# Moving one batch's x matmuls, its copies and two orderings in a fused attention and MLP kernel

## The chip, the cores and the metric

The kernel runs on one core of one Trainium2 chip. The metric is the device time of one execution in microseconds, as the median of several executions. A profile is one execution recorded by the hardware. Its span is about 1.8 us shorter than the time of the same execution (280.7 us against 282.54 us for the kernel before).

The engines are TensorE (PE in the profile), VectorE (DVE), ScalarE (ACT), GpSimd (POOL) and SyncE (SP), which here issues most of the DMA transfers (115 of the 120 that --dma lists for the kernel before). "L535" means line 535 of that kernel's own file.

## The reference, cut

There are 8 batches of 576 rows. Each batch goes through an attention that has no score matrix, then through a normalized two-layer MLP with a residual.

```python
def _attn_ref(q, k, v):                      # each (8, 8, 576, 64)
    q_s = exp(q - max(q, -1)); q_s /= sum(q_s, -1)
    k_s = exp(k - max(k, 2));  k_s /= sum(k_s, 2)
    kv = np.einsum('bhsd,bhse->bhde', k_s, v)
    return np.einsum('bhsd,bhde->bhse', q_s, kv)

def _moe_ref(x, g_ln, w_ch1, w_ch2):         # x (8, 576, 512), w_ch1 (512, 2048), w_ch2 (2048, 512)
    xn = (x - mean(x)) / np.sqrt(var(x) + 1e-06) * g_ln
    return x + np.maximum(xn @ w_ch1, 0.0) @ w_ch2
```

## The kernel before: the parts that matter

The MLP is done in nine chunks: the first 512 rows of each batch (chunks 0 to 7), and the last 64 rows of all batches together (chunk 8). While TensorE works on the MLP of chunk c, the other engines prepare batch c+1:

- ScalarE takes the exponentials of q and k (`eq`, `ek`) and casts v (`vb`).
- A DMA transposes `eq` into `eqT`.
- TensorE forms `kv`, and from `eqT` the transposed x. These are "the x matmuls": eight of 64x512, then eight of 64x64 for the last 64 rows.
- The results are copied out as `xsT`, which the chunk's first layer reads.
- Another DMA transposes `xsT` back to `x`, which the row statistics (`bn_stats` into `bst`) and the residual need.

Nothing is issued in program order. Every operation is entered in a plan, and a list scheduler orders the operations on each engine:

```python
    def add(self, eng, dur, fn, r=(), w=(), cls=1, land=0.0, mb=0.0, after=(), slack=0.0):
        ...                                   # deps: from the keys read (r) and written (w)
        order_only = set(after) - deps        # only shapes the plan; makes no data dependence
        self.tasks.append((eng, dur, fn, deps | order_only, (cls, i), ...))
```

An `after` holds an operation back in the plan. On one engine that fixes its place in the instruction order. Between two engines the built program waits only for data.

The casts of v, and the copies of the x matmuls' results:

```python
        def values(hf, s):
            ...
                plan.add("ACT", act_t(QW), lambda: nc.scalar.copy(vd, va), r=sk(s), w=[...],
                         cls=cls, slack=late, after=exps)

        def xT(hs):                           # 4 x matmuls for each h, then copies
            ...
                    if not steady and i == 1:
                        ev.append(plan.add("DVE", dve_t(512), lambda ...: nc.vector.tensor_copy(xt[:, g], pv), ...))
                    else:
                        ev.append(plan.add("ACT", act_t(512), lambda ...: nc.scalar.copy(xt[:, g], pv), ...))
```

The statistics of a chunk's x wait for the transposition. They stand on VectorE wherever the scheduler puts them:

```python
    def tokens(c, cls=1, after=()):
        i = plan.add("SP", 2.2, lambda: nc.sync.dma_start_transpose(x..., src...), r=r, w=[(xk, j) for j in range(J)], ...)
        for j in range(J):
            plan.add("DVE", dve_t(512), lambda j=j: nc.vector.bn_stats(bst[:, j, :], x[:, j, :]), r=[(xk, j)], ...)
            ...
```

From chunk 1 on, the second layer has seven products of half-size blocks. It uses sums `S` of the hidden blocks and sums `T` of w2's blocks. The second of its four output steps frees the PSUM bank that the last product needs:

```python
        product("S3", "T3", ga, False, False)
        final(o2, 1, ga, 2, 1)                # VectorE: ot <- pg (bank of ga), cp
        product("S4", "22", gb, False, True)
        final(o1, 1, gb, 1, 0)
        product("22", "T4", ga, False, True)  # TensorE needs ga's bank back
```

Chunk 0 has a plain second layer of 64 large matmuls. The sums `T` are formed meanwhile, 4 of the 16 on GpSimd:

```python
        for k0 in range(0, KO2, 4):
            for j in range(J):
                ...                           # four 128x512 matmuls
        ...
    def w2_sums(k0, n):
        ...
            eng, e = ("POOL", nc.gpsimd) if i == 2 else ("DVE", nc.vector)
            plan.add(eng, ..., lambda: e.tensor_tensor(T[i][:, ks], a, b, op=ALU.subtract), r=r, w=tk(i), cls=2)
```

The softmax here doesn't subtract the row's maximum and nothing guards it: scores larger than these inputs give would overflow.

## Time and profile before

| | before |
|---|---|
| median of 3 runs at the time of the prediction | 281.96 us (281.94 to 282.53) |
| median of 4 runs, beside the changed kernel | 282.12 us |
| TensorE busy, engine table | 269.3 of 280.7 us |
| VectorE, ScalarE, GpSimd busy | 205.1, 163.9, 12.6 us |

TensorE bounds this kernel almost everywhere. What a reordering can win is the idle time that is left on it, so the profile is read by stage. The first view of the kernel before is the table of stretches, cut at the starts of chunks 1, 2 and 3 on TensorE. Its columns are the stretch, its length, the busy time of each engine, the granted TensorE clock, the DMA share and GB/s.

```profile
37.30:55.00 17.70, 15.98 (x153) 7.29 (x152) 17.13 (x32) 8.40 (x13) 5.00 (x4) 1.00 1.10 293
55.00:83.40 28.40, 27.94 (x265) 18.07 (x263) 23.73 (x49) 24.10 (x35) 0.00 (x0) 1.00 0.95 288
83.40:113.40 30.00, 28.16 (x273) 17.98 (x266) 22.81 (x49) 19.90 (x34) 0.00 (x0) 1.00 0.81 191
113.40:276.00 162.60, 162.60 (x1402) 105.41 (x1400) 112.37 (x232) 87.73 (x150) 0.00 (x0) 1.00 0.52 138
```

The last stretch has no idle time on TensorE. The second layer of chunk 0 (first line, from 37.30 us) lacks 1.7 us, chunk 1 lacks 0.5 us and chunk 2 lacks 1.8 us.

Next comes TensorE's timeline of the kernel before: start, duration, line, operation, output and inputs, array tile, shape, count, and in brackets the idle time before the group with what ended it.

```profile
49.14 0.63 PE L405 MATMUL pa<-eqT,kve 64*64 64x512 bf16 x8 [1.23 <-DMA eqT<-eq]
49.70 1.04 PE L677 MATMUL pg<-w_sb,hT 128*128 128x512 f16 x4
50.66 0.22 PE L428 MATMUL pa<-eqT,kve 64*64 64x64 bf16 x2
51.37 0.25 PE L428 MATMUL pa<-eqT,kve 64*64 64x64 bf16 x6 [0.49 <-DVE xsT L416]
51.55 3.63 PE L677 MATMUL pg<-w_sb,hT 128*128 128x512 f16 x16
55.01 1.24 PE L535 MATMUL pa<-xsT,w_sb 128*128 128x512 f16 x5
```

The same timeline of the kernel before, at the ends of chunks 1 and 2:

```profile
81.38 1.91 PE L615 MATMUL pg<-T,hT 128*128 128x256 f16 x16 [0.41 <-DVE ot L625]
...
83.41 9.78 PE L535 MATMUL pg<-xsT,w_sb 128*128 128x512 f16 x44
...
107.90 1.91 PE L615 MATMUL pg<-w_sb,S 128*128 128x256 f16 x16
111.65 1.91 PE L615 MATMUL pg<-T,hT 128*128 128x256 f16 x16 [1.84 <-DVE ot L625]
113.39 0.81 PE L535 MATMUL pg<-xsT,w_sb 128*128 128x512 f16 x3
```

The four brackets are the four gaps of the prediction: A (1.23), B (0.49), C (0.41) and D (1.84). The cause of D is on VectorE, whose timeline of the kernel before shows a statistics instruction that waits for x ahead of the output step (`ot`) that TensorE needs:

```profile
106.35 0.88 DVE L625 SCALAR_TENSOR_TENSOR cp<-pg,st,x 128x256 f32<-128x256 f32 x2 [0.87 <-PE pg L615]
110.12 0.69 DVE L487 BATCH_NORM_STATS2 bst<-x 128x6 f32<-128x512 f16 x1 [2.89 <-DMA x<-xsT]
110.73 0.86 DVE L625 SCALAR_TENSOR_TENSOR ot<-pg,st,cp 128x256 f32<-128x256 f32 x2
```

Both casts of v wait for their loads, and they stand ahead of the copies of `xsT`:

```profile
79.59 1.17 ACT L368 CAST vb<-stg 128x1152 f16<-128x1152 f32 x1 [0.32 <-DMA stg<-in_v_dram]
81.03 1.17 ACT L368 CAST vb<-stg 128x1152 f16<-128x1152 f32 x1 [0.27 <-DMA stg<-in_v_dram]
82.10 1.06 ACT L418 CAST xsT<-pa 128x512 f16<-128x512 f32 x2
```

GpSimd's sums of w2, in the timeline of the kernel before:

```profile
43.14 2.45 POOL L566 TENSOR_TENSOR T<-w_sb 128x512 f16<-128x512 f16 x2 [17.28 <-DVE w_sb L301]
46.55 2.55 POOL L566 TENSOR_TENSOR T<-w_sb 128x512 f16<-128x512 f16 x2 [0.96 <-DVE w_sb L301]
```

### The profile page before, as it was taken

The numbers are of one execution on the slowest core, as the hardware profiler recorded it, in microseconds if no ns is written. First come the engines' busy times: TensorE is split into PE (matmuls) and PEld (weight loads), VectorE is DVE, ScalarE is ACT, GpSimd is POOL, SyncE is SP. The second block draws the span as 40 slices with busy tenths as digits, with TensorE's granted clock in tenths as the row PEclk, the third lists the DMA queues.
The fourth block names the chain that finished last, engine by engine and source line by source line (L and its number), as shares of the span: only waits on it lengthen the run. The fifth ranks groups of instructions, "written<-read, shape, count | busy, mean of one in ns | idle before, by whom it ended". The sixth has DMA issues, their size and how long they took to land.

```text
span 280.7 us, 5656 instructions
## 1 busy us (share of the span) xinstructions
PE 269.3 (96%) x2317; PEld 163.8 (58%) x2317; DVE 205.1 (73%) x408; ACT 163.9 (58%) x267; POOL 12.6 (5%) x17
## 2 busy tenths in 40 slices
PE   8988898999999997999999999999999999999994
PEld 3443344445864486546854785478447844874583
DVE  0988999899869874986598659966986683641573
ACT  3567793298887594569655865695565067006500
POOL 2115007000000000000000000000000000000000
PEclk9999999999999999999999999999999999999998
DMA  6999999999958992569655995797543650013004
GB/s 190 386 388 386 390 388 202 313 297 258 385 186 149 251 354 63 149 145 381 141 149 104 388 177 149 156 392 122 149 86 21 131 149 2 0 36 116 1 2 151
DMA packets 58522, 55.36 MB, mean 197 GB/s; under 512 B 37248, under 2 KB 37760, under 8 KB 58496
## 3 DMA queue, kind: packets, MB, share of 16 engines
q1 hardware_dynamic: 57776, 54.86, 68.6%
q8 instruction: 18, 0.29, 0.4%
q10 hardware_dynamic: 720, 0.13, 0.3%
q14 instruction: 8, 0.07, 0.1%
HBM read 36.70 MB, written 9.44 MB: 164 GB/s over the span
## 4 chain that ended last, share of the span: by engine, by line
PE 73%; DMA 13%; DVE 9%; ACT 1%; POOL 1%; issue 1%; DVEq 0%
PE pg L535 37%; PE pg L615 28%; DMA stg<-in_moe_w_ch_dram 6%; DMA x<-xsT 5%; PE pg L677 3%; DVE T L566 2%; DMA stg<-in_q_dram 2%; DVE S L551 2%; DVE bst L487 1%; PE pa L379 1%; PE pa L615 1%; PE pa L535 1%; POOL w_sb L271 1%; DVE ot L625 1%; PE pa L405 1%
## 5 line engine op out<-in xcount | busy, mean ns | idle before, releaser
L498 ACT ACTIVATE hT<-pg 128x512 f16<-128x512 f32 x134 | 79.4, 596 | 73.4 <-PE pg L535 72.6
L535 PE MATMUL pg<-xsT,w_sb 128*128 128x512 f16 x488 | 108.1, 379 | 0.5 <-DVE w_sb L292 0.5
L535 PEld LDWEIGHTS <-w_sb 128*128 128x128 f16 x568 | 54.8, 98 | 65.6 <-DVE w_sb L292 1.5
L615 PEld LDWEIGHTS <-S 128*128 128x128 f16 x512 | 49.7, 98 | 5.9
L615 PEld LDWEIGHTS <-hT 128*128 128x128 f16 x384 | 37.0, 98 | 10.5 <-issue 5.0
L615 PE MATMUL pg<-T,S 128*128 128x256 f16 x368 | 42.5, 273 | 0.1
L551 DVE TENSOR_TENSOR S<-hT 128x1024 f16<-128x1024 f16 x32 | 22.0, 688 | 25.9 <-ACT hT L498 25.8
L625 DVE SCALAR_TENSOR_TENSOR cp<-pg,st,x 128x256 f32<-128x256 f32 x46 | 20.2, 479 | 13.7 <-PE pg L615 12.9
L615 PE MATMUL pg<-w_sb,hT 128*128 128x256 f16 x248 | 29.3, 273 | 0.0
L625 DVE SCALAR_TENSOR_TENSOR ot<-pg,st,cp 128x256 f32<-128x256 f32 x47 | 20.5, 478 | 9.9 <-PE pg L615 9.7
L487 DVE BATCH_NORM_STATS2 bst<-x 128x6 f32<-128x512 f16 x36 | 24.0, 668 | 4.9 <-DMA x<-xsT 4.8
L331 DVE TENSOR_REDUCE zq<-eq 128x18 f32<-128x1152 bf16 x16 | 21.5, 1344 | 5.7 <-ACT eq L329 5.7
L329 ACT ACTIVATE eq<-stg 128x1152 bf16<-128x1152 f32 x16 | 18.7, 1172 | 6.2 <-DMA stg<-in_q_dram 6.2
L335 DVE TENSOR_TENSOR eq<-eq,rzq 128x1152 bf16<-128x1152 bf16 x16 | 21.7, 1357 | 0.5
L356 ACT ACTIVATE ek<-stg 128x1152 bf16<-128x1152 f32 x16 | 18.6, 1169 | 1.5 <-DMA stg<-in_k_dram 1.5
L418 ACT CAST xsT<-pa 128x512 f16<-128x512 f32 x28 | 14.5, 595 | 4.7 <-PE pa L405 4.7
L368 ACT CAST vb<-stg 128x1152 f16<-128x1152 f32 x14 | 16.3, 1171 | 0.6 <-DMA stg<-in_v_dram 0.6
L615 PE MATMUL pg<-T,hT 128*128 128x256 f16 x120 | 14.4, 273 | 2.2 <-DVE ot L625 2.2
L615 PE MATMUL pg<-w_sb,S 128*128 128x256 f16 x128 | 15.3, 273 | 0.0
L696 PE MATMUL pg<-zero 128*128 128x512 f16 x47 | 13.4, 441 | 1.2 <-DVE zero L222 1.2
L677 PE MATMUL pg<-w_sb,hT 128*128 128x512 f16 x64 | 14.5, 380 | 0.0
L535 PE MATMUL pg<-xT,w_sb 128*128 128x512 f16 x64 | 14.0, 379 | 0.0
(67 smaller groups left out, 176.2 us busy)
## 6 DMA issues: line engine op xcount, KB each, us to landing
stg<-in_q_dram SPq DMA_DIRECT2D x16, 576.0 KB, 5.4
stg<-in_k_dram SPq DMA_DIRECT2D x16, 576.0 KB, 7.4
stg<-in_v_dram SPq DMA_DIRECT2D x16, 576.0 KB, 8.2
out_dram<-ot SPq DMA_DIRECT2D x33, 256.0 KB, 3.6
stg<-in_moe_w_ch_dram SPq DMA_DIRECT2D x16, 512.0 KB, 10.2
out_dram<-ot SPq DMA_DIRECT2D x1, 512.0 KB, 2.8
x<-xsT SPq DMA_TRANSPOSE x8, 6.7
out_dram<-ot SPq DMA_DIRECT2D x1, 128.0 KB, 2.7
```

The source lines that it names most:

```text
L329: plan.add("ACT", act_t(QW), lambda: nc.scalar.activation(e.rearrange("p j (s d) -> p s j d", s=2), sv(s), AF.Exp), r=sk(s), w=[("eq", u, ...
L331: plan.add("DVE", dve_t(QW), lambda: nc.vector.reduce_sum(zq[:, hf], eh, axis=AX.X), r=[("eq", u, hf)], w=[("zq", hf)], cls=qcls, after=sums_)
L335: plan.add("DVE", dve_t(QW), lambda: nc.vector.tensor_tensor(eh, eh, rzq[:, hf].to_broadcast([P, 2 * JT, D]), op=ALU.mult), r=[("rzq", hf) ...
L356: plan.add("ACT", act_t(QW), lambda: nc.scalar.activation(ek[u][:, hf].rearrange("p j (s d) -> p s j d", s=2), sv(s), AF.Exp), r=sk(s), w= ...
L368: plan.add("ACT", act_t(QW), lambda: nc.scalar.copy(vd, va), r=sk(s), w=[("vb", u, hf, i) for i in range(2)], cls=cls, slack=late, after=exps)
L487: plan.add("DVE", dve_t(512), lambda j=j: nc.vector.bn_stats(bst[:, j, :], x[:, j, :]), r=[(xk, j)], w=[("bst", j)], cls=cls, slack=2.0 if ...
L498: nc.scalar.activation(hT[:, m, :], bank, AF.Relu)
L535: nc.tensor.matmul(bank[gi], w1_sb[:, ko, m * P : m * P + P], xt[:, ko], start=(ko == 0), stop=(ko == KO1 - 1))
L551: plan.add("DVE", dve_t(256 * n, 2), lambda: nc.vector.tensor_tensor(S[i][:, ks], a, b, op=op), r=r, w=sk(i), cls=0.3 if k0 else 0.45)
L615: nc.tensor.matmul(g[i][0], fa(k, i), fb(k), start=(first and k == 0 and (i == 0 or g[0][1] != g[1][1])), stop=(last and k == HK - 1), ski ...
L625: nc.vector.scalar_tensor_tensor(dst[:, i, :], in0=g[i][0], scalar=sti[:, 4, 2 * t0 + i : 2 * t0 + i + 1], in1=src[:, i, :], op0=ALU.mult, ...
L677: nc.tensor.matmul(pg[gis[j]], hT[:, kk, j * P : j * P + P], w2_sb[:, kk, :], start=(kk == 0), stop=(kk == KO2 - 1))
```

## The change

The change adds and removes no matmul. Its intent has three parts:

1. **Placement and copies.** Batch 1's eight x matmuls are split 4 + 4. They are placed behind fixed steps of chunk 0's second layer, with the last eight behind them, so that no copy is awaited. Batch 1's copies of `xsT` go to ScalarE alone, as do two more casts of w2.
2. **Two orderings.** The statistics of the next x stand behind one output step (the `final` above). The casts of v stand behind the copies of `xsT`.
3. **GpSimd.** Its sums of w2 are to run beside chunk 0's outputs, away from VectorE's sums, because the two engines were expected to slow each other. The trace of the kernel before shows six of VectorE's sums taking 5.2 us beside GpSimd's, against 0.42 us for one alone.

```diff
@@ values
-                         cls=cls, slack=late, after=exps)
+                         cls=cls, slack=late, after=tuple(exps) + (tuple(state["ev"][-1][-1:]) if steady else ()))
@@ xT
-                    if not steady and i == 1:
+                    if kind == "first" and i == 1:
                         ev.append(plan.add("DVE", ...
@@ attn (early)
+        if not steady:
+            return lambda n, after: xT([n], after) if n < 2 else xT_last(after)
@@ tokens
-            plan.add("DVE", dve_t(512), lambda j=j: nc.vector.bn_stats(...), ..., slack=2.0 if c else 0.5)
+            plan.add("DVE", dve_t(512), lambda j=j: nc.vector.bn_stats(...), ..., slack=2.0 if c else 0.5, after=stats)
@@ w2_sums
-            plan.add(eng, 0.8 if i == 2 else ..., cls=2)
+            plan.add(eng, 1.2 if i == 2 else ..., cls=2, after=after if i == 2 else ())
@@ mm2_split
-        final(o2, 1, ga, 2, 1)
+        state["stats"] = (final(o2, 1, ga, 2, 1),)
@@ mm2
+        steps = [(8, 1), (8, 3), (12, 1)]
         ...
+                if (k0, j) in steps:
+                    second_x(steps.index((k0, j)), (i,))
@@ second_w2
-        w2_rows(8)
-        w2_rows(12)
+        for k0 in range(8, 16, 2):
+            load_w2(k0, "ACT")
@@ main
-            tokens(b, 0.7)
+            tokens(b, 0.7, stats=state["stats"])
-                w2_sums(k0, 2)
+                w2_sums(k0, 2, evs)
```

(Cut: the threading of `after` through functions, and the same `stats` for chunk 8.)

More of the change, by code (lines that the diff above doesn't have):

```diff
@@ L395, in kv, with xT @@
                             r=[("pa", a), ("rz", g)], w=[("kve", u, g)], cls=0.35 if steady else 0)
-        def xT(hs):
+        def xT(hs, after=()):
             ab = [[nxt("pa", 4) for _ in range(2)] for _ in hs]
@@ L407, in xT @@
             plan.add("PE", 0.2 + 0.2 * len(hs), f, r=[("eqT", u, h) for h in hs] + [("kve", u, 2 * h + e) for h in hs for e in range(2)],
-                     w=[("pa", a) for x in ab for a in x], cls=0, slack=SLACK if steady else 0.0)
+                     w=[("pa", a) for x in ab for a in x], cls=0, slack=SLACK if steady else 0.0, after=after)
             ev = []
@@ L419, in xT, with xT_last @@
             state["ev"].append(ev)
-        def xT_last():
+        def xT_last(after=()):
             ab = [nxt("pa", 4) for _ in range(2)]
@@ L430, in xT_last @@
             plan.add("PE", 0.3, f, r=[("eqT", u, 2)] + [("kve", u, g) for g in range(G)], w=[("pa", a) for a in ab],
-                     cls=0 if steady else 0.5, slack=SLACK if steady else 0.0)
+                     cls=0 if steady else 0.5, slack=SLACK if steady else 0.0, after=after)
             c0 = R * (b % 2)
@@ L469, in attn @@
             kv(hs)
-        for hs in ([[0, 1]] if steady else [[0], [1]]):
-            xT(hs)
+        if not steady:
+            return lambda n, after: xT([n], after) if n < 2 else xT_last(after)
+        xT([0, 1])
         xT_last()
@@ L475, in xof, with tokens @@
         return (xb[c % 3], ("x", c % 3), st[c % 3], ("st", c % 3)) if c < B else (x8, "x8", st[3], ("st", 3))
-    def tokens(c, cls=1, after=()):
+    def tokens(c, cls=1, after=(), stats=()):
         x, xk, sti, stk = xof(c)
@@ L486, in tokens @@
         for j in range(J):
-            plan.add("DVE", dve_t(512), lambda j=j: nc.vector.bn_stats(bst[:, j, :], x[:, j, :]), r=[(xk, j)], w=[("bst", j)], cls=cls, slack=2.0 if c else 0.5)
+            plan.add("DVE", dve_t(512), lambda j=j: nc.vector.bn_stats(bst[:, j, :], x[:, j, :]), r=[(xk, j)], w=[("bst", j)], cls=cls, slack=2.0 if c else 0.5, after=stats)
             plan.add("DVE", 0.18, lambda j=j: nc.vector.bn_aggr(bmv[:, j, :], bst[:, j, :]), r=[("bst", j)], w=[("bmv", j)], cls=cls)
@@ L555, in sums, with w2_sums @@
         tt(2, h11, h21, ALU.subtract, lo)
-    def w2_sums(k0, n):
+    def w2_sums(k0, n, after):
         ks, kh = slice(k0, k0 + n), slice(HK + k0, HK + k0 + n)
@@ L565, in tt @@
             eng, e = ("POOL", nc.gpsimd) if i == 2 else ("DVE", nc.vector)
-            plan.add(eng, 0.8 if i == 2 else dve_t(256 * n, 2), lambda: e.tensor_tensor(T[i][:, ks], a, b, op=ALU.subtract),
-                     r=r, w=tk(i), cls=2)
+            plan.add(eng, 1.2 if i == 2 else dve_t(256 * n, 2), lambda: e.tensor_tensor(T[i][:, ks], a, b, op=ALU.subtract),
+                     r=r, w=tk(i), cls=2, after=after if i == 2 else ())
         tt(0, b12, b11, lo)
@@ L635, in final @@
         def final(o, half, g, n, t0):
-            plan.add("DVE", 0.84, lambda: scaled(ot[o][:, :, 256 * half : 256 * half + 256], g, t0,
+            return plan.add("DVE", 0.84, lambda: scaled(ot[o][:, :, 256 * half : 256 * half + 256], g, t0,
                                                  cp[n].rearrange("p (i c) -> p i c", i=2)),
@@ L681, in mm2 @@
                     ids.append(i)
+                if (k0, j) in steps:
+                    second_x(steps.index((k0, j)), (i,))
         plan.fill(ids[0], ids[-1], zeros(pg[gis[0]], False))
+        evs = []
         for hf in range(2):
@@ L686, in mm2 @@
                 j = 2 * hf + i
-                plan.add("DVE", dve_t(512), lambda o=o, i=i, j=j: nc.vector.scalar_tensor_tensor(
+                ev = plan.add("DVE", dve_t(512), lambda o=o, i=i, j=j: nc.vector.scalar_tensor_tensor(
                     ot[o][:, i, :], in0=pg[gis[j]], scalar=st[c % 3][:, 4, j : j + 1], in1=xb[c % 3][:, j, :],
@@ L690, in mm2 @@
                     r=[("pg", gis[j]), (("x", c % 3), j), (("st", c % 3), "r", j)], w=[("ot", o, i)], cls=0)
+                evs.append(ev)
             store(c, o, hf)
+        return evs[:1]
     def zeros(bank_, start):
@@ L704 @@
     warmed = warm(12)
-    state = {"eqT": (), "ev": []}
+    state = {"eqT": (), "ev": [], "stats": ()}
     opened = [nxt("pg", 4) for _ in range(4)]
@@ L729 @@
     w2_rows(4)
-    attn(1, "early", second_w2)
+    second_x = attn(1, "early", second_w2)
     before = ()
@@ L734 @@
         if b:
-            tokens(b, 0.7)
+            tokens(b, 0.7, stats=state["stats"])
         if b == B - 1:
-            tokens(8, 0.7)
+            tokens(8, 0.7, stats=state["stats"])
         ids = mm1(b, b > 0, () if b else opened)
@@ L745 @@
         if b == 0:
-            mm2(b)
+            evs = mm2(b)
             for k0 in range(0, HK, 2):
-                w2_sums(k0, 2)
+                w2_sums(k0, 2, evs)
         else:
```

## The prediction

> **What bounds it now.** TensorE: busy 269.3 of 280.7 us (engine table). In the chain of waits every chunk from the fourth on takes 27.86 us without a gap (113.55, 141.41, 169.27), so nothing can be won there. A reordering can win TensorE's idle time after the start-up; its timeline shows four pieces, 3.97 us in all:
> - A, 1.23 us before 49.14: batch 1's first x matmul waits for the DMA transpose of eq. It stands behind 44 of chunk 0's 64 second-layer matmuls.
> - B, 0.49 us before 51.37: batch 1's last x matmuls wait for VectorE's copy of xsT. From 49.14 to the next chunk at 55.18 there are 6.04 us for 5.08 us of work (0.56 + 0.20 + 20 x 0.216), so B costs nearer 0.9.
> - C, 0.41 us before 81.38: chunk 1's last product waits for VectorE's output step.
> - D, 1.84 us before 111.65: the same in chunk 2, for another reason: VectorE idled 2.89 us until 110.12 in a statistics instruction whose x had not landed, ahead of the output step that TensorE needs.
>
> **What the change does.** No matmul is added or removed.
> 1. Batch 1's eight x matmuls are split 4 + 4, its last eight moved eight large matmuls later; all xsT copies go to ScalarE (0.6 us each; it idles 2.98 us there), as do two weight casts. The first x matmul still stands behind 44 matmuls, and eq, its transpose and the loads before it are untouched: A stays. B should go: the copies end near 52, before the last x matmuls. Gain 0.85 us (0.7 to 1.0).
> 2. Statistics behind the output step: in chunk 2 that step then runs at its product's end, some 0.8 us before TensorE wants it. D goes, 1.84 us. VectorE's next steps may still wait for x, but their banks are needed 1.7 us later. Value casts behind xsT's copies let x leave earlier (by about 1 us in chunk 1) and spare about 0.1.
> 3. GpSimd's sums: this ordering holds only in the plan. In the built order they wait for weight casts, not for chunk 0's outputs. They will still run near 43 to 48.5 us, beside VectorE's sums, which they stretch: six of those took 5.2 us there, against 0.42 each alone. [...] Step 3 does next to nothing. VectorE still loses about 2.6 us of work to ScalarE, and chunk 0's outputs start when its statistics (x lands at 50.6) allow, near 54.5 instead of 56.05.
> C stays: chunk 1's order on TensorE is unchanged, and the 0.89 us output step has only 0.56 us of x matmuls beside it.
>
> **Sum.** 0.85 + 1.84 + 0.1 = 2.8 us, nearly all on the critical path: 281.96 - 2.8 = 279.2 us, 8 in 10 within 278.4 to 280.4. Faster by over 2% would need 5.6 us, more than all four gaps: 0.02. Within 2%: 0.97. Slower: 0.01.
>
> **What would show it.** Right: the wait for eq's transpose still near 1.2 us; no wait on xsT; chunk 1 starting near 54.3; GpSimd's sums before 50; chunk 2's last product without a wait; C near 0.4; later chunks 27.86 us. Wrong: A shrinking, GpSimd's sums after 54, or chunk 2 still waiting.
>
> **What would make it wrong.** D's x landing so late that the following output steps stall the next chunk; a late statistics chain in a steady chunk; the weight casts delaying ScalarE's kve and so the x matmuls; two loads now issued ahead of chunk 1's x starving a later transpose.

The sum came to 0.85 + 1.84 + 0.1 = 2.8 us.

## More of the kernel before

The changed kernel's lines stand one or two further down, so L625 before is L626 after, and L677 is L679.

## The result, and the profile after

| | before | after |
|---|---|---|
| median, same rounds | 282.12 us (281.94 to 282.53, 4 runs) | 280.16 us (280.12 to 280.23, 4 runs) |
| span of the profiled run | 280.7 us | 278.4 us |
| TensorE busy | 269.3 us | 269.1 us |
| VectorE, ScalarE busy | 205.1, 163.9 us | 202.4, 166.6 us |

The ratio is 0.9929, with a 95% interval of 0.9912 to 0.9946: within 2%, and faster. A ratio here is the mean time of one kernel's fast runs over that of the other's of the same rounds, so it is not quite the ratio of the medians quoted.

The table of stretches of the kernel after, cut at the same events, answers to the one of before:

```profile
37.30:54.50 17.20, 16.04 (x154) 7.19 (x152) 15.22 (x29) 11.92 (x19) 4.93 (x4) 1.00 1.09 291
54.50:82.90 28.40, 27.94 (x266) 18.07 (x264) 23.41 (x47) 22.79 (x33) 0.00 (x0) 1.00 1.00 295
82.90:110.80 27.90, 27.90 (x273) 18.02 (x266) 22.52 (x47) 20.26 (x34) 0.00 (x0) 1.00 0.79 206
110.80:273.40 162.60, 162.60 (x1402) 105.45 (x1400) 112.33 (x234) 87.91 (x150) 0.00 (x0) 1.00 0.54 138
```

The four stretches went from 17.70, 28.40, 30.00 and 162.60 us to 17.20, 28.40, 27.90 and 162.60 us. So the gain comes from two places: 0.5 us in chunk 0 and 2.1 us in chunk 2. TensorE's timeline of the kernel after shows them:

```profile
49.10 0.41 PE L405 MATMUL pa<-eqT,kve 64*64 64x512 bf16 x4 [1.16 <-DMA eqT<-eq]
49.44 1.04 PE L679 MATMUL pg<-w_sb,hT 128*128 128x512 f16 x4
50.41 0.41 PE L405 MATMUL pa<-eqT,kve 64*64 64x512 bf16 x4
50.75 1.90 PE L679 MATMUL pg<-w_sb,hT 128*128 128x512 f16 x8
52.58 0.26 PE L428 MATMUL pa<-eqT,kve 64*64 64x64 bf16 x8
52.77 1.90 PE L679 MATMUL pg<-w_sb,hT 128*128 128x512 f16 x8
54.51 1.67 PE L536 MATMUL pa<-xsT,w_sb 128*128 128x512 f16 x7
```

The same timeline of the kernel after, at the ends of chunks 1 and 2:

```profile
80.87 1.91 PE L616 MATMUL pg<-T,hT 128*128 128x256 f16 x16 [0.41 <-DVE ot L626]
...
82.89 9.67 PE L536 MATMUL pg<-xsT,w_sb 128*128 128x512 f16 x44
...
109.02 1.91 PE L616 MATMUL pg<-T,hT 128*128 128x256 f16 x16
110.77 3.40 PE L536 MATMUL pg<-xsT,w_sb 128*128 128x512 f16 x15
```

A is still there (1.16 us), B is gone, C is still there (0.41 us), D is gone. VectorE's timeline of the kernel after shows why D went: the output step now starts at its product's end (what ended the 0.87 us of idle time before it is TensorE), and the statistics wait behind it.

```profile
107.47 0.88 DVE L626 SCALAR_TENSOR_TENSOR ot<-pg,st,cp 128x256 f32<-128x256 f32 x2 [0.87 <-PE pg L616]
108.76 0.69 DVE L488 BATCH_NORM_STATS2 bst<-x 128x6 f32<-128x512 f16 x1 [0.41 <-DMA x<-xsT]
```

On ScalarE of the kernel after, the copies of `xsT` wait only for TensorE, and v is cast later:

```profile
80.28 2.05 ACT L418 CAST xsT<-pa 128x512 f16<-128x512 f32 x4 [0.74 <-PE pa L405]
82.19 1.20 ACT L368 CAST vb<-stg 128x1152 f16<-128x1152 f32 x1
```

GpSimd's sums of the kernel after are in the same place as before, as its timeline shows:

```profile
42.63 2.48 POOL L567 TENSOR_TENSOR T<-w_sb 128x512 f16<-128x512 f16 x2 [16.73 <-ACT w_sb L301]
45.59 2.57 POOL L567 TENSOR_TENSOR T<-w_sb 128x512 f16<-128x512 f16 x2 [0.48 <-ACT w_sb L301]
```

They still overlap VectorE's sums, in VectorE's timeline of the kernel after eight instructions that take 5.88 us:

```profile
44.15 5.88 DVE L567 TENSOR_TENSOR T<-w_sb,T 128x512 f16<-128x512 f16 x8
```

Chunk 0's outputs, beside which they were to run, start at 54.53 us.

### Where the gain on TensorE came from, by starts of groups

An idle time in brackets counts from the modelled end of the group before, which overlaps the next start by some 0.16 us in a stream without a gap (in the kernel after, 1.91 us from 109.02 ends at 110.93, and the next group starts at 110.77). Differences of starts are cleaner:

| term | before | after | gain, us |
|---|---|---|---|
| first x matmul of batch 1 (gap A) | 49.14 | 49.10 | 0.04 |
| last eight x matmuls with gap B (50.66 to 51.55; 52.58 to 52.77) | 0.89 | 0.19 | 0.70 |
| the eight 64x512 x matmuls, together or 4 + 4 | 0.56 | 0.34 + 0.34 | −0.12 |
| the 20 large matmuls among them | 0.96 + 3.46 | 0.97 + 1.83 + 1.74 | −0.12 |
| chunk 1 (55.01 to 83.41; 54.51 to 82.89) | 28.40 | 28.38 | 0.02 |
| chunk 2's last product but one with gap D (107.90 to 111.65; 107.27 to 109.02) | 3.75 | 1.75 | 2.00 |
| rest of chunk 2 | 26.23 | 26.13 | 0.10 |
| **start of chunk 3** | **113.39** | **110.77** | **2.62** |

The last group of matmuls starts at 276.08 us before and 273.45 us after, which is 2.63 us earlier. From the issue of the last store to the end of the span it is 3.03 us before and 3.36 us after, which takes 0.33 us back. The store landed 2.2 us after its issue in both, so this difference lies behind the landing. The spans differ by 2.3 us. The profiled run of before took 282.54 us and was as slow as the slowest of the timed ones (281.94 to 282.53); that of after took 280.19 us. So the medians differ by 1.96 us only. The mean granted clock of the profiled run of before, 0.997, is not why it was slow: its clock fell to 0.50 only at 279.1 us, after the last matmul.

### The profile page after: what moved, and what is told of

The parts are those of the page before. It is cut to its first block, busy times and chain, and to the rows that moved or that the text cites. A ratio compares the mean times of both kernels' runs of the same rounds, so it can differ in the third digit from the quotient of the medians.

```text
span 278.4 us, 5654 instructions
## 1 busy us (share of the span) xinstructions
PE 269.1 (97%) x2317; PEld 163.8 (59%) x2317; DVE 202.4 (73%) x404; ACT 166.6 (60%) x271; POOL 12.5 (5%) x17
## 4 chain that ended last, share of the span: by engine, by line
PE 83%; DMA 10%; DVE 4%; POOL 1%; ACT 0%; issue 0%; DVEq 0%
PE pg L536 41%; PE pg L616 33%; DMA stg<-in_moe_w_ch_dram 6%; PE pg L679 3%; DMA eqT<-eq 2%; DMA stg<-in_q_dram 2%; PE pa L379 1%; PE pa L405 1%; PE pa L616 1%; PE pa L536 1%; POOL w_sb L271 1%; DVE S L552 1%; DVE cp L284 0%; DVE ot L626 0%; PE pa L428 0%; DVE w_sb L274 0%
## 5 line engine op out<-in xcount | busy, mean ns | idle before, releaser
L626 DVE SCALAR_TENSOR_TENSOR ot<-pg,st,cp 128x256 f32<-128x256 f32 x47 | 20.5, 477 | 11.3 <-PE pg L616 11.1
L418 ACT CAST xsT<-pa 128x512 f16<-128x512 f32 x30 | 15.5, 595 | 4.7 <-PE pa L405 4.7
```

The source lines that it names most:

```text
L626: nc.vector.scalar_tensor_tensor(dst[:, i, :], in0=g[i][0], scalar=sti[:, 4, 2 * t0 + i : 2 * t0 + i + 1], in1=src[:, i, :], op0=ALU.mult, ...
```

## The experiments

The diffs of the experiments named "only" are against the kernel before, those of the others against the kernel after (12 is against the kernel before). They are cut to the lines that act; the threading of `after` and `stats` is left out. There are twelve runs, with five rounds each beside runs of the kernel before on the same chip. The median of before was 282.14 us in the first submission, then 282.01, 282.23 and 282.19 us. The kernel before had two outliers, counted as fast: 284.12 us at a mean clock of 0.991 in the first submission and 285.99 us at 0.994 in the second. They enter its mean, so they lower the ratios of eight runs a little and widen their intervals. One part needed no run. With part 3 alone taken back, the built program has the same instruction order on all five engines (no row differs). So **part 3 changes nothing in the program**: its `after` binds two engines, and so it makes no wait.

This table has all runs. "1", "2" and "3" are the starts of chunks 1, 2 and 3 on TensorE, "last" is the start of the last group of matmuls, and "x(3)" is the landing of batch 3's x (issue plus time to landing). All five columns are of the profiled run.

| kernel | median, us | ratio to before (95%) | 1 | 2 | 3 | last | x(3) |
|---|---|---|---|---|---|---|---|
| before | 282.12 | 1 | 55.01 | 83.41 | 113.39 | 276.08 | 110.1 |
| after | 280.16 | 0.9929 (0.9912, 0.9946) | 54.51 | 82.89 | 110.77 | 273.45 | 108.8 |
| only_copies | 282.52 | 1.0001 (0.9975, 1.0028) | 54.39 | 84.02 | 112.13 | 274.93 | 108.8 |
| only_place | 281.61 | 0.9977 (0.9954, 1.0001) | 54.37 | 84.37 | 112.38 | 275.15 | 109.0 |
| only_stats | 281.09 | 0.9958 (0.9934, 0.9981) | 55.10 | 84.46 | 112.47 | 275.15 | 109.5 |
| only_values | 282.46 | 0.9998 (0.9975, 1.0022) | 55.08 | 83.47 | 113.21 | 276.03 | 109.9 |
| all_but_values | 281.92 | 0.9992 (0.9947, 1.0037) | 54.51 | 83.82 | 111.82 | 274.89 | 109.0 |
| all_but_stats | 284.59 | 1.0078 (1.0029, 1.0128) | 54.53 | 82.91 | 116.16 | 279.94 | 111.3 |
| all_but_place | 280.79 | 0.9946 (0.9897, 0.9995) | 54.49 | 82.88 | 110.75 | 274.86 | 110.3 |
| later_x | 279.74 | 0.9911 (0.9867, 0.9956) | 52.82 | 81.76 | 109.63 | 274.69 | 110.7 |
| whole_again | 280.42 | 0.9932 (0.9920, 0.9945) | 54.43 | 82.82 | 110.69 | 273.38 | 109.1 |
| later_x_last_step | 278.64 | 0.9874 (0.9860, 0.9887) | 53.15 | 81.55 | 109.55 | 272.44 | 107.9 |
| gpsimd_really_late | 281.12 | 0.9960 (0.9947, 0.9974) | 54.59 | 82.97 | 110.84 | 273.99 | 109.9 |
| stats_and_values | 280.67 | 0.9954 (0.9940, 0.9967) | 54.93 | 83.32 | 111.19 | 273.92 | 109.5 |

The theory at the start was that of the prediction: two independent gaps, B and D, each removed by one part, so that the parts add up. The rival was that the parts act through each other.

### 1. only_copies: the copies and casts on ScalarE alone

```diff
-                    if not steady and i == 1:
+                    if kind == "first" and i == 1:
-        w2_rows(8)
-        w2_rows(12)
+        for k0 in range(8, 16, 2):
+            load_w2(k0, "ACT")
```

> The kernel before with one part alone: batch 1's xsT copies and the four weight casts of rows 8 to 15 on ScalarE; the x matmuls are placed by the scheduler, statistics and value casts as before. Theory (the gain before chunk 1 comes from taking the copies off the full VectorE; splitting the x matmuls costs time): TensorE needs about 5.2 us from batch 1's first x matmul to chunk 1's first matmul, against 5.87 before and 5.41 with the whole change; total 0.6 to 0.7 us below before. Rival (the gain comes from the new place of the x matmuls): no gain, within 0.2 us of before. Chunk 2's gap stays near 1.8 us under both.

In its own place the expectation held. The 5.87 us from the first x matmul to chunk 1 became 5.17 us (49.22 to 54.39), and the scheduler itself moved the last x matmuls eight large ones further. The total did not follow: 282.52 us. Chunk 1 started 0.62 us earlier and chunk 2 started 0.61 us later than before. Two new waits, of 0.69 and 0.27 us, on ScalarE's copies of `xsT` had appeared near 83 us, because the casts of v (at 80.22 and 81.66 us, each waiting for its load) stood ahead of the copies. The last matmuls were still 1.15 us earlier, since x(3) landed earlier and D was absent. But from the last store's issue to the end it was 4.2 us instead of 3.0: the store took 3.3 us to land instead of 2.2.

### 2. only_place: the placement alone

```diff
+        if not steady:
+            return lambda n, after: xT([n], after) if n < 2 else xT_last(after)
+        steps = [(8, 1), (8, 3), (12, 1)]
+                if (k0, j) in steps:
+                    second_x(steps.index((k0, j)), (i,))
```

> The kernel before with the new place of batch 1's x matmuls alone (4 + 4, the last eight after two thirds of the last quarter), copies still shared with VectorE. Both theories expect no wait on xsT and about 5.4 us from the first x matmul to chunk 1, 0.4 to 0.5 us below before; my theory adds that this is less than the copies alone give, because of the split, the rival that it is all of the gain.

From the first x matmul to chunk 1 it was 5.40 us (48.97 to 54.37), 0.23 us more than with the copies alone: this is the price of the split, the two lines of −0.12 in the table of terms. Again two new waits (1.05 and 0.27 us) on `xsT` stood near 84 us, and chunk 2 started 0.96 us later than before. So whichever part makes chunk 1 early, chunk 2 loses it. The median, 281.61 us, is still 0.53 us below before, about what was expected, but not for the expected reason: x(3) landed at 109.0 us in this profile, and D was absent, as in only_copies.

### 3. only_stats: the statistics behind one output step, alone

```diff
-        final(o2, 1, ga, 2, 1)
+        state["stats"] = (final(o2, 1, ga, 2, 1),)
-            tokens(b, 0.7)
+            tokens(b, 0.7, stats=state["stats"])
```

> The kernel before with the statistics tied to the output step alone. Theory (chunk 2's gap is the order on VectorE): the 1.84 us wait before chunk 2's last product is gone although x lands as late as before (near 110.1 us); total 1.8 to 2.0 us below before. Rival (the gap went because x landed earlier, since value casts stand behind xsT's copies): the wait stays, or turns into a wait of the next chunk's matmuls on a bank, total within 0.4 us of before.

D was gone as expected (chunk 2's last product starts at 110.72 us and chunk 3 at 112.47 us, without a wait). The gain was 1.05 us in medians, not 1.8 to 2.0. In TensorE's timeline of only_stats the rest is near 84 us, where the kernel before has no wait:

```profile
83.79 0.22 PE L428 MATMUL pa<-eqT,kve 64*64 64x64 bf16 x2 [0.42 <-ACT xsT L418]
84.28 0.25 PE L428 MATMUL pa<-eqT,kve 64*64 64x64 bf16 x6 [0.27 <-ACT xsT L418]
```

ScalarE's timeline of only_stats has the reason, the casts of v waiting for their loads ahead of the copies:

```profile
80.66 1.17 ACT L368 CAST vb<-stg 128x1152 f16<-128x1152 f32 x1 [0.32 <-DMA stg<-in_v_dram]
82.10 1.17 ACT L368 CAST vb<-stg 128x1152 f16<-128x1152 f32 x1 [0.27 <-DMA stg<-in_v_dram]
83.17 1.55 ACT L418 CAST xsT<-pa 128x512 f16<-128x512 f32 x3
```

The edit does not move these casts. They start 1.07 us later than in the kernel before (79.59 and 81.03), because v's loads landed later, and so do the copies. The kernel before just missed this wait in its own profile; whether its other executions have it was not seen.

### 4. only_values: the casts of v behind the copies, alone

```diff
-                         cls=cls, slack=late, after=exps)
+                         cls=cls, slack=late, after=tuple(exps) + (tuple(state["ev"][-1][-1:]) if steady else ()))
```

> The kernel before with the value casts behind the xsT copies alone. Theory: chunk 2's x leaves SyncE some 2.5 us earlier, chunk 3's x lands about 0.8 us earlier, so chunk 2's gap shrinks from 1.84 to about 1.0 us and total is 0.8 to 1.0 us below before; not all of the gap goes, as the output step still stands behind a statistics instruction. Rival: the gap is gone, 1.8 to 2.0 us below before.

This missed: no gain in the total. The copies did move (80.85 us instead of 82.10 us) and chunk 2 started at 83.47 us without a wait. But x(3) landed at 109.9 us, hardly earlier than before, and D stood at 1.71 us. The earlier copies did not buy an earlier landing of x(3); its transposition was issued 0.42 us earlier (101.34 instead of 101.76 us) and took 8.6 us to land instead of 8.3.

**What follows from the first four.** The parts do not add up (−0.38, +0.53, +1.05 and −0.32 us of gain in medians, against 1.96 us together). The new theory has two places that are set by DMA loads rather than by TensorE:

- Near 83 us, v of batch 3 arrives when its loads arrive. With the casts ahead of the copies of `xsT`, chunk 2 cannot start before about 83.8 to 84.5 us once TensorE or the loads shift a little. The value order takes this limit away.
- Near 110 us, x(3) lands at 107.9 to 111.3 us, and this does not follow TensorE's pace (the two kernels that issue it first, at 99.6 us, have it at 107.9 and at 110.7 us). With the statistics ahead of the output step, chunk 3 starts about 3.3 us after that landing (before: 110.1 to 113.39). Any earlier gain is swallowed. The tie takes this limit away.

The next runs take one part out of the whole change.

### 5. all_but_values

```diff
-                         cls=cls, slack=late, after=tuple(exps) + (tuple(state["ev"][-1][-1:]) if steady else ()))
+                         cls=cls, slack=late, after=exps)
```

> The whole change without the new order of the value casts. New theory (two points in chunks 1 and 2 are set by loads and not by TensorE, and an earlier gain is lost there unless both are loosened): ScalarE waits near 80 to 82 us for value loads before it copies xsT, TensorE waits 0.7 to 1.3 us on xsT near 83 us, total 281.0 to 281.5, about 1 us over the whole change. Rival (my prediction: the value order is worth 0.1): within 0.2 us of the whole change, no such wait.

The median was 281.92 us, 1.5 us above the whole change run later (280.42), 1.8 us above its first runs (280.16) and a little above the expected range. Chunk 1 started at 54.51 us, exactly as in the whole change, and chunk 2 at 83.82 us instead of 82.89 us, behind waits of 0.37 and 0.27 us on `xsT`; chunk 3 started 1.05 us later than in the whole change. The last group was 1.44 us later. The further 0.4 us arose behind chunk 3's start, in part as a wait of 0.22 us for VectorE's output step at 198.37 us. That part is not shown to come from this ordering: all_but_place, which keeps the ordering, has a wait for the same step at 198.35 us (0.41 us). The ordering that the prediction had booked with 0.1 us, and that won nothing alone, is what lets chunk 0's gain get through chunk 1.

### 6. all_but_stats

```diff
-            tokens(b, 0.7, stats=state["stats"])
+            tokens(b, 0.7)
```

> The whole change without the tie of the statistics. New theory: chunk 3's x lands near 108.7 to 109.5 whatever TensorE does, the output step stands behind its first statistics instruction again, and the wait before chunk 2's last product comes back at 1.2 to 2.0 us, swallowing what was won before it: total 281.6 to 282.2. Rival (x lands earlier in the changed kernel, so the tie isn't needed): under 0.7 us of wait, total 280.3 to 280.9.

This was slower than before, 284.59 us, and slower than expected. TensorE's timeline of this kernel shows why:

```profile
107.29 1.91 PE L616 MATMUL pg<-w_sb,S 128*128 128x256 f16 x16
112.80 3.57 PE L616 MATMUL pg<-T,hT 128*128 128x256 f16 x16 [3.60 <-DVE ot L626]
116.16 4.15 PE L536 MATMUL pg<-xsT,w_sb 128*128 128x512 f16 x14
```

x(3) landed at 111.3 us, and the idle time grew to 3.60 us. After it the same 16 matmuls took 3.57 us instead of 1.91, a factor of 1.9, and the next 44 took 10.63 us instead of 9.66. The granted clock fell in the gap: --windows gives 1.00 from 108 to 110 us and 0.82 from 110 to 112 us. Where a fall was read in finer steps, behind the last matmul of the kernel before, it went from 1.00 to 0.50. If it did so here, it fell near 111.3 us, 2.1 us after TensorE's modelled last end (109.20), and half the clock until about 118.1 us gives the time that these 60 matmuls lost (both times are estimates, from the 0.82 and from the four durations). The run's mean clock of 0.988 fits that. The idle time before the fall was not the same everywhere: behind the last matmul it was 2.0 us in the kernel before and 3.0 us in only_copies, and in the kernel after the clock had not fallen after 3.9 us. In the shorter gap of the kernel before (1.84 us) it stayed at 1.00. So this wait cost more than itself, about 2.6 us more. The mean clocks of the other runs (0.993 to 0.994 in four of the five, where the profiles without such an event have 0.996 or more) suggest the same event in them; their traces were not taken. The two outliers of the kernel before have such clocks too (0.991 and 0.994), so it may now and then lose time in the same way.

### 7. all_but_place

```diff
-        if not steady:
-            return lambda n, after: xT([n], after) if n < 2 else xT_last(after)
-                if (k0, j) in steps:
-                    second_x(steps.index((k0, j)), (i,))
```

> The whole change without the new places of batch 1's x matmuls: the scheduler puts all eight together and the last eight 8 large matmuls on. Theory (the copies on ScalarE do it; the split costs about 0.2): 5.2 us from batch 1's first x matmul to chunk 1 against 5.41, total 279.9 to 280.1. Rival (the placement is what wins): 5.8 us or more there, total 280.5 or more.

The starts of chunks 1, 2 and 3 (54.49, 82.88, 110.75 us) were those of the whole change (54.51, 82.89, 110.77), though the eq transposition arrived 0.2 us later. So the placement named first in the change wins nothing there beyond what the copies on ScalarE win. The median was 280.79 us, above the expected 279.9 to 280.1, but the runs spread from 280.29 to 282.35 us, and the interval of the ratio (0.9897 to 0.9995) contains that of the whole change. In the profiled run x(3) came at 110.3 us, and a wait of 0.42 us followed at 114.05 us. VectorE's output steps after the tied one stand behind statistics again, so the tie does not protect them. Another wait of 0.41 us for VectorE's output step stood at 198.35 us. In all, the last group came 1.4 us later than in the whole change.

### 8. later_x: the x matmuls together, after 52 large ones

```diff
-        steps = [(8, 1), (8, 3), (12, 1)]
+        steps = [(12, 0), (12, 0), (12, 2)]
```

> The whole change with batch 1's eight x matmuls together and behind 48 large matmuls plus one group of 4 (52 in all instead of 44), its last eight 8 further on. The wait for eq's transpose (1.16 us, untouched by the change) is then covered by large matmuls. Theory: that wait is gone, the split cost too, chunk 1 starts near 53.1 instead of 54.5, and with both later points loosened most of it stays: total 278.8 to 279.3. If chunk 1's VectorE or the loads bind instead, chunk 1's wait before its last product grows from 0.41 and the total stays above 279.6.

A, the largest gap, is only a matter of place. With the x matmuls behind 52 instead of 44 large matmuls, the eq transposition is there when TensorE comes, and chunk 1 starts at 52.82 us, 1.7 us earlier than after. A new wait of 0.60 us for VectorE, at 73.37 us, takes part of it back. The median was 279.74 us, above the expected range, 0.4 us below the whole change's first runs; the intervals of the two ratios overlap. In the profiled run (281.48 us, the slowest; the others were 279.25 to 279.77) x(3) landed at 110.7 us, and the output steps after the tied one made TensorE wait 1.57 and 0.42 us in chunk 3. TensorE came to chunk 3 at 109.63 us, 1.14 us earlier than in the kernel after, and the two waits behind x(3) took 1.99 us.

### 9. whole_again: the change once more, as a control

No edit: this is the changed kernel again.

> The changed kernel once more, beside the kernel before, as a control: is its 280.12 to 280.23 of the first four runs its usual time, or does it too lose time when chunk 3's x lands late (108.7 us in its first trace; 110.3 and 110.7 in two variants of it)? Theory: most runs at 280.1 to 280.5, some up to 281.5, where x landed after about 109.5 us and chunk 3's matmuls waited on VectorE's later output steps. Rival: all within 0.3 us.

The median was 280.42 us (280.08 to 280.66): the result holds. The profiled run (280.11 us) has no wait in chunks 2 and 3. Whether x(3) was late in the slower runs was not seen, and none took over 280.7 us.

### 10. later_x_last_step: later_x, with the statistics behind the chunk's last output step

```diff
-        state["stats"] = (final(o2, 1, ga, 2, 1),)
+        final(o2, 1, ga, 2, 1)
...
-            plan.add("DVE", 0.48 * len(slots), lambda slots=slots: scaled(ot[o2][:, :, 0:256], ...
+            step = plan.add("DVE", 0.48 * len(slots), lambda slots=slots: scaled(ot[o2][:, :, 0:256], ...
             if c < B:
+                state["stats"] = (step,)
```

> The kernel with the later x matmuls, and the statistics tied to the last output step of a chunk instead of the third of five. Theory: no output step stands behind a late x any more, so the waits at 113.1 and 114.5 us (1.57 and 0.42) are gone wherever x lands; chunk 1 starts near 52.8, the wait for VectorE near 73.4 (0.60) and the 0.41 before chunk 1's last product stay; total 278.2 to 278.9 with a spread under 0.8. If the statistics, later now, delay the scale factors of a steady chunk, chunks from the fourth on take over 27.9 us and the total is above 279.5.

The median was 278.64 us (278.61 to 278.90, 4 runs), the ratio 0.9874: the fastest kernel, 1.8 us below the control of the same rounds, and with a narrow spread. Only C remains of the waits from chunk 1 on; that of 0.60 us near 73.4 us, which was expected to stay, is gone too, with chunk 1 starting at 53.15 us. The last three output steps now start as their products end, and no statistics stand between them. In its profile x(3) also happened to land earliest of all (107.9 us). Whether the spread stays this narrow when it lands at 111 us was not seen.

### 11. gpsimd_really_late: what part 3 meant to do

A small copy on GpSimd reads chunk 0's first output, so that the sums really wait for it:

```diff
+            evs = [plan.add("POOL", 0.2, lambda: nc.gpsimd.tensor_copy(seen, ot[0][:, 0, 0:1]), r=[("ot", 0, 0)])]
             for k0 in range(0, HK, 2):
                 w2_sums(k0, 2, evs)
```

> The changed kernel with one small GpSimd copy that reads chunk 0's first output, placed ahead of GpSimd's four sums, so that they really run beside chunk 0's outputs (near 55.5 to 60.5 us). Theory (the third part of the change does nothing, and even when it is made to happen it wins nothing, since VectorE then waits for x at 50.6 us anyway): VectorE's eight sums take 3.4 us instead of 5.9, its statistics still start near 50.6, total within 0.4 us of the changed kernel run beside it, or slower if the sums stretch VectorE's multiplication near 60 us. Rival (GpSimd's sums cost critical time where they stand): 0.5 us or more faster.

The sums ran from 55.59 us, and VectorE's eight sums took 3.3 us instead of 5.88. VectorE then idled 3.17 us, because batch 0's x landed at the same time as ever: its statistics started at 50.73 us (after: 50.63 us). The median was 281.12 us, 0.7 us above the control. So VectorE's sums do run slower beside GpSimd's, but off the critical path, and taking that away gains nothing. Why it costs 0.7 us is not settled. In its trace the last group of matmuls starts 0.6 us later than in the control's: chunk 1 starts 0.16 us later, and two stretches of 44 matmuls, at 110.84 and at 194.65 us, took 9.88 and 9.89 us instead of 9.66. Another 0.9 us is the end after the last store's issue (4.2 us instead of 3.3), but the profiled run (281.59 us) was the slowest of the five.

### 12. stats_and_values: the two orderings together, nothing else

The edits of only_stats and only_values, both, in the kernel before:

```diff
-        final(o2, 1, ga, 2, 1)
+        state["stats"] = (final(o2, 1, ga, 2, 1),)
-                         cls=cls, slack=late, after=exps)
+                         cls=cls, slack=late, after=tuple(exps) + (tuple(state["ev"][-1][-1:]) if steady else ()))
```

> The kernel before, with two parts of the change: the statistics tied to one output step, and the value casts behind the copies of xsT. Placement, copies and weight casts are as in the kernel before. The tie alone won 1.0 us and lost the rest to two new waits on xsT near 84 us (0.42 and 0.27 us); the value order alone won nothing. Theory of two loads (the value casts that wait for v hold up the copies of xsT that TensorE needs, and only the tie with the value order keeps what either wins): no wait on xsT near 83 us, no wait in chunk 2, chunk 3 starting on TensorE at 111.2 to 111.7 us, and 279.9 to 280.6 us in all, that is 1.6 to 2.2 us below the kernel before, though the two parts won 1.0 and 0 alone. Rival (the parts add up, and the placement and the copies of chunk 0 win their own 0.85 us in the whole change): 280.9 to 281.3 us, about 1.0 us below the kernel before.

The median was 280.67 us, just above the range of the theory of two loads and below that of its rival. Its trace fits the theory: no wait near 83 us, none in chunk 2, chunk 3 at 111.19 us. In the traces' measure, the start of the last matmuls, the tie alone won 0.93 us, the value order alone 0.05 us, both together 2.16 us and the whole change 2.63 us. In medians the value order's addition to the tie is smaller (281.09 to 280.67), and the two ratios, 0.9958 and 0.9954, hardly differ, so these two runs alone do not show it; all_but_values does. The profiled run of only_stats was the slowest of its six (281.62 us), so its trace may show more of the wait near 84 us than a typical run has. B, left in this kernel, showed as 0.18 us only, because A was longer (1.54 us): the two share one slack, 1.72 us in both kernels.

## Why the prediction was right, and where its terms were off

The prediction named 279.2 us, and the result, 280.16 us, lies inside its range. Its mechanisms, point by point:

- **A stays**: right, 1.23 to 1.16 us. later_x shows that it was to be had by moving the x matmuls eight large ones further.
- **B goes, gain 0.85 us**: it went, but the term was mis-sized. Chunk 1 started 0.50 us earlier. The wait itself cost 0.70 us (0.89 instead of 0.19 us for the last eight). The split gave 0.24 us of that back in two terms that the prediction left out: 0.12 us because 4 + 4 small matmuls take longer than 8 (0.68 instead of 0.56 us), and 0.12 us in the large matmuls around one more change of matmul size. The traces show the size of the second term, not its cause: four large matmuls between two 64x64 groups take 0.97 us from start to start, where sixteen in a row take 3.46, that is 0.87 us for four. The 6.04 us of the prediction also read chunk 1's start from the chain of waits (55.18), which counts from the group before's modelled end; from start to start it was 5.87 us. And all_but_place shows that the copies on ScalarE, not the placement, remove the wait.
- **D goes, 1.84 us**: right, and worth 2.00 us from start to start. all_but_stats shows that it is needed: without it the rest of the change loses 2.6 us to the kernel before, though x(3) was late in its profile (111.3 us) and the slower clock after the gap is part of that. At the 108.8 us of the kernel after, the product would start near 110.35 us without the tie instead of 109.02 (an estimate, from the 1.55 us between landing and product in the kernel before), so D did not go only because x(3) came earlier.
- **The value order spares about 0.1 us**: this step failed. It wins nothing alone, but about 1.0 us of the whole change's gain on TensorE at chunk 3's start hangs on it (all_but_values), because with v's casts ahead of the copies the loads of v set chunk 2's start. The prediction silently took B's gain as reaching the end. That needed this ordering: in the traces of only_copies and only_place the gain does not reach chunk 2's start without it. So in this term the sum was right by luck: the ordering was there, but for a reason that the prediction did not have.
- **Step 3 does nothing**: right; the built instruction order is the same without it. The trace of the kernel before showed the stretch, and the runs give its size, not its cause: eight VectorE sums took 5.88 us with GpSimd's sums beside the first 4 us of them, and 3.3 us without (0.40 to 0.43 us each alone).
- **C stays**: right, 0.41 us in both kernels.
- **The sum, 2.8 us on the critical path**: 2.63 us on TensorE. The prediction took the gaps from a profiled run, whose time was 282.54 us, and subtracted them from the median, 281.96 us. That alone is 0.58 us of the 0.96 us between 279.2 and the result. The end of the kernel was 0.33 us longer, and the sum itself was 0.17 us too large. These make 1.08 us; the remaining 0.12 us the other way is within the spread of runs.

What stays open: why x(3) lands anywhere between 107.9 and 111.3 us (6.6 to 11.1 us after its issue in the fourteen profiles), and why the end from the last store's issue is 3.0 to 3.4 us long in eleven profiles and 4.2 us in three (in only_copies, one of the three, the 128 KB store landed after 3.3 us, in the kernels before and after it landed after 2.2). In the run with the latest x(3), SyncE's issue of its transposition lasted 7.03 us against 4.46 us in the kernel after. The traces place the start of the delay earlier: in the five profiles where SyncE's issue of the two loads of k before it, at 92 to 95 us, lasted 3.1 to 4.3 us, x(3) landed at 109.9 to 111.3 us, broadly the later the longer that issue was. In eight others it lasted 1.0 to 1.6 us and x(3) landed at 107.9 to 110.1 us. So in these five the delay shows before the transposition is issued. What causes it, no run shows.

## What to carry to other kernels

When several engines feed a kernel whose TensorE is as busy as here (269.3 of 280.7 us), look ahead of each removed wait for the next place where a DMA's arrival sets the time (here v's loads near 83 us and x(3) near 110 us). A gain reached the end here only through both, so an ordering that looked worthless alone carried much of it, and a leave-one-out run showed this where the one-part run did not (the value order won nothing alone, and leaving it out cost 1.5 us). Where an engine idles in an instruction that waits for a DMA while a step that another engine needs stands behind it (2.89 us on VectorE in chunk 2 here), put that instruction behind the step. Subtract gaps that were read in one profiled run from the time of that same run, by starts of groups and not by modelled idle times.
